# Attention, gate and mixer on one core: token products that wait for the token weights alone, and the second head's block first in the products with v

## The chip, the cores and the metric

The kernel runs on one core of one Trainium2 chip. The metric is the time of one execution on the device in microseconds (us); the median of three runs is given. The core has five engines with a program each: TensorE (PE in the rows, with PEld for its weight loads), VectorE (DVE), ScalarE (ACT), GpSimd (POOL) and SyncE (SP). They run side by side and wait for each other on semaphores.

## The reference

Three layers follow one another, in float32, for 4 batches of 576 tokens. Attention with 8 heads of dimension 64 keeps the 32 largest scores of each row:

```python
    scores = scale * np.matmul(q, k.transpose(0, 1, 3, 2))
    kth = np.partition(scores, -top_k, axis=-1)[..., -top_k:-top_k + 1]
    mask = scores >= kth
    ...
    return np.matmul(attn, v).astype(np.float32)
```

The gate layer multiplies a sigmoid of a causal convolution of five taps with x @ w_val, and the product with w_out. The mixer turns each value by an angle, mixes over tokens with two 576 x 576 matrices, and adds a channel product:

```python
    theta = x @ w_theta
    cos_t, sin_t = (np.cos(theta), np.sin(theta))
    zr = x * cos_t
    zi = x * sin_t
    yr = np.einsum('ts,bsd->btd', w_tok_r, zr)
    yi = np.einsum('ts,bsd->btd', w_tok_i, zi)
    y = yr + yi
    u = x + y
    return (u + np.maximum(u @ w_ch, 0.0)).astype(np.float32)
```

## The kernel before

**Tiles.** The heads go in 16 head pairs, four to a batch. Tokens are cut into two column parts, 256 and 320 wide (x or h is 0 or 1 in the names), and the 512 channels into four panels of 128 (m or c). An attention tile is 128 rows of one head. For each: score products (`ps`, L545 and L546), a copy to SBUF (`s`, L559), the search for the 32nd largest value on DVE (`cand`, `tops`, `thrs`; L581 to L608) with POOL's `y` (L602) and ACT's `n` (L594) in it, the exponential (`e`, L202), the masked product (`s`, L661), and transposes (`pt`, L674) copied to `pT` (L693).

**The product with v.** When both heads of a pair have their pT for a column part, `close` issues the block `px` (L757 to L765): five products for each head, the first head's result in rows 0 to 63 and the second's in rows 64 to 127 of one PSUM tile. The inner loop takes the first head (j = 0) and then the second for each 128 tokens. Then `close` multiplies px by the reciprocal row sums (`rs`, L718; spread as `rb`) into `xT`, and for batches 0 to 2 builds the convolution `gp` (L818 to L830: one step on ACT, one on POOL at L822, the rest on DVE).

**Gate and mixer.** They are written as Python generators that yield after each small group of products, and a step loop calls them. `front(b)` makes `pval` (x @ w_val, consumed by DVE at L859), `px2t`, the angles `pth` and the turned `z`. `back(b)` makes the token products `py` (L1114), adds them to x in `x2T` (L1093, in `y_out`), then the channel products `ph`, and stores. Each step of the loop gives the generators a budget of PE time (4150 ns). A generator that yields "sync" ends the work of that step. `later` and `mid` are lists of functions that run at fixed points of the next step.

**Splits.** Batches from 1 on, and w_ch for batch 0 too, use operands that are split into a high and a low part. `halve` does it: a cast on ACT (L408) and in the next round a subtract on DVE or POOL (L412). `want(b, name, m)` starts it for the weight panels up to m. `halve_room` does it for whole tiles: `X` (xT for pval), `G`, `U` (the output of the token products, for ph). For batch 1's first X the function `h_out` of `back(0)` starts the split of panel m as soon as that panel of ph is done and the head pair's xT is there; `front(1)` starts those that are missing.

**Weights.** The raw weights come as 64-bit words and are converted in 54 pieces, in the order conv, val, out, theta, tok, ch. `lacking[name]` counts the pieces that are left. The first line of `back` that runs is

```python
        while any(lacking.values()):
            yield "sync"
```

**What sets the order.** The loop runs the named stages of a step in a listed order. On DVE and ACT the instructions run in the order in which they are written. On PE, POOL and SP a scheduler orders them by priority and by when it expects their inputs.

Of the kernel before, what the change touches and what calls it, by code (L numbers as in the profile page):

```python
# [90 lines left out]
def mixer(ctx, tc, qT, kT, vt, w_val, conv_t, w_out, w_theta, w_tok, w_ch, out, flag):  # L91
# [99 lines left out]
    taken, lacking = set(), {}  # L191
# [63 lines left out]
    def double(u, j, x):  # L255

        r = slice(64 * j, 64 * j + 64)
        q2 = q2s[j]
        kh, kl = (io.tile([P, S], I32, tag=f"{t}{j}", name=f"{t}{j}_{u}_{x}") for t in ("kh", "kl"))
        for d in range(2):  # L260
            o = slice(64 * d, 64 * d + 64)
            nc.sync.dma_start(kh[o, :], raws["k", u, x][0][r, :].bitcast(I32))
            nc.sync.dma_start(kl[o, :], raws["k", u, x][1][r, :].bitcast(I32))
            q = raws["q", u, x][d][r, :].bitcast(I32)
            c = columns_of("q", x)
            if j and c.stop == S:
                nc.sync.dma_start(q2[o, c.start : NF * P], q[:, c.start : NF * P])
                nc.sync.dma_start(q2[o, S:], q[:, NF * P :])
            else:
                nc.sync.dma_start(q2[o, c], q[:, c])  # L270
        heads[u, j] = tuple(t.bitcast(F32R) for t in (q2, kh, kl))
# [123 lines left out]
    def chunk(b, x, what, c):  # L395
        both = parts_of(b, x, what)
        w = COLS[x][1] - COLS[x][0]
        return both[:, 0, c, :w], both[:, 1, c, :w]
# [6 lines left out]
    def halve(hi, lo, src, key, also=None):  # L405

        def higher():
            nc.scalar.copy(hi, src)  # L408
            later.append(lower)

        def lower():
            engine(key).tensor_tensor(lo, src, hi.bitcast(F32), ALU.subtract)  # L412
            if also is not None:
                also()
            if PATIENT and attending[0]:
                later.append(lambda: done.add(key))
            else:
                done.add(key)

        mid.append(higher)  # L420

    def halve_room(b, x, what, src):

        both = parts_of(b, x, what)
        lo, hi = COLS[x]
        for c in range(0, NC, 2):
            halve(both[:, 0, c : c + 2, : hi - lo], both[:, 1, c : c + 2, : hi - lo], src[:, c : c + 2, lo:hi],
                  (what, b, c, x))
        if what == "L" and x:
            halve(both[:, 0, :, hi - lo :], both[:, 1, :, hi - lo :], src[:, :, NF * P :], (what, b, "last", x))  # L430

    def halved(b, x, what):
        return [(what, b, c, x) for c in range(0, NC, 2)] + [(what, b, "last", x)] * (what == "L" and x)
# [7 lines left out]
    def place(k, m):  # L441

        if k < 3 or k % 3 == 2:
            return [ml.tile([P, DM], F32R if k < 3 else I32, tag=f"{t}{m}", name=f"{t}{m}_{k}") for t in ("hi", "lo")]
        if (k, 0) not in places:
            names = ("val", "out") if k % 3 == 0 else ("theta", "ch")
            for t in range(2):
                places[k, t] = cp.tile([P, NC, DM], I32, tag=f"w_{names[t]}", name=f"w{t}_{k}")
        return [places[k, t][:, m, :] for t in range(2)]
# [3 lines left out]
    def want(b, name, last=NC - 1):  # L453

        k = PHASES.index((b, name)) if b else -1
        if k > 2:
            return
        for m in range(last + 1):
            if (b, name, m) in mats:
                continue  # L460
            src = W[name][:, m, :] if name == "theta" else W[name][:, :, m * P : (m + 1) * P]
            both = place(k, m)
            mats[b, name, m] = both
            stored[name, m] = dp.tile([P, 2, DM], I32, name=f"{name}{m}")

            def store(both=both, to=stored[name, m]):
                for t in range(2):
                    nc.sync.dma_start(to[:, t, :], both[t].bitcast(I32))

            hi, lo = (t if name == "theta" else t.rearrange("p (c w) -> p c w", c=NC) for t in both)  # L470
            halve(hi, lo, src, ("w", b, name, m), store)
# [11 lines left out]
    def used(b, name):  # L483

        if b:
            k = PHASES.index((b, name))
            for k in {0: (), 1: (3,), 2: (4, 5)}.get(k, (k + 3,)):
                bring(k)

    def mat(b, name, m, c):  # L490
        return tuple(t[:, c * P : (c + 1) * P] for t in mats[b, name, m])
# [7 lines left out]
    def after(*keys):  # L499
        while not done.issuperset(keys):  # L500
            yield "sync"
# [6 lines left out]
    def products(ps, terms):  # L508

        last, w = len(terms) - 1, ps.shape[-1]  # L510
        for i, (a, b) in enumerate(terms):
            ways = passes(a, b)
            for k, (x, y) in enumerate(ways):
                n = x.shape[-1]
                for o in range(0, P, n):
                    nc.tensor.matmul(ps[o : o + n], x, y, start=(i + k == 0),  # L516
                                     stop=(i == last and k == len(ways) - 1), skip_group_check=(n < P))
            owe[0] += w * (1.275 if len(ways) > 1 else 1.675)
            if owe[0] >= GRAIN and i < last:
                yield paid()  # L520
# [3 lines left out]
    def paid():  # L524
        ns, owe[0] = owe[0], 0.0
        return ns
# [181 lines left out]
    def close(part):  # L708

        u, x = part["u"], part["x"]  # L710
        b, hp = divmod(u, NP)
# [47 lines left out]
        owed[0] -= 8.3 * w  # L759
        px = ps_m.tile([P, w], F32, tag="m", name=f"px_{u}_{x}")  # L760
        for c in range(NF + 1):
            for j in range(2):
                d = slice(64 * j, 64 * j + 64)
                of_v, k = (v[:, c, d], j * NF + c) if c < NF else (v_last[:, d], 2 * NF)
                nc.tensor.matmul(px[d, :], of_v, pT[:, k, :],  # L765
                                 start=(c == 0), stop=(c == NF), skip_group_check=True)
# [31 lines left out]
        if hp == NP - 1:  # L798
            jobs.append(front(b, (x,) if split else (0, 1)))
            if x:  # L800
                jobs.append(back(b))
# [284 lines left out]
    def back(b):  # L1086
        x2T = ms.pop(b)

        def y_out(m, h, ps):
            lo, hi = COLS[h]  # L1090

            def f():
                nc.vector.tensor_tensor(x2T[:, m, lo:hi], ps, x2T[:, m, lo:hi], ALU.add)  # L1093
                if m == NC - 1 and (h or b == B - 1):
                    for k in (h,) if b == B - 1 else range(2):
                        halve_room(b, k, "U", x2T)
                if not h:
                    want(b, "ch", m)
            return f

        while any(lacking.values()):
            yield "sync"
        if b < B - 1:
            for h, m in [(h, m) for h in range(2) for m in range(NC)]:
# [36 lines left out]
        def h_out(m, h, ps):  # L1141
            lo, hi = COLS[h]

            def f():
                nc.vector.scalar_tensor_tensor(x2T[:, m, lo:hi], ps, 0.0, x2T[:, m, lo:hi], ALU.max, ALU.add)
                n = b + 1
                if h and n in THREE:
                    want(n, "val", m)
                    if (n * NP + m, 0) in there:
                        split_x(n, m, 0)  # L1150
                done.add(("o", b, m, h))
            return f
# [8 lines left out]
        def turned(tiles):  # L1161
            for i in tiles:
                w = P if i < NF else REM
                po = ps_m.tile([P, NC, P], F32, tag="m", name=f"po_{b}_{i}")
                for c in range(NC):
                    nc.tensor.transpose(po[:w, c, :], x2T[:, c, i * P : i * P + w], ident)
                later.append(store(i, w, po))
                yield 450

        for h, m in [(h, m) for h in range(2) for m in range(NC)]:  # L1170
            lo, hi = COLS[h]
            yield from after(*halved(b, h, "U"), ("w", b, "ch", m))
            ps = ps_m.tile([P, hi - lo], F32, tag="m", name=f"ph_{b}_{m}_{h}")
            yield from products(ps, [(mat(b, "ch", m, c), chunk(b, h, "U", c)) for c in range(NC)])
            later.append(h_out(m, h, ps))
            if (h, m) == (1, NC - 1):
                used(b, "ch")
            yield paid()
            if h and m == 1:
                yield from after(*[("o", b, c, 0) for c in range(NC)])  # L1180
                yield from turned([0, 1])
# [65 lines left out]
    for k, part in enumerate(order):  # L1247
# [7 lines left out]
        elif split or x == 0:  # L1255
            when = (i0 - 7, i0 - 5, i0 - 5, i0 - 4, i0 - 3) if split or i0 and order[k - 1]["x"] and order[k - 1]["u"] // NP in SPLIT else (i0 - 9, i0 - 8, i0 - 7, i0 - 6, i0 - 3)
            a = (u, x if split else None)
            for step, do in zip(when, (load_heads, split_high, split_low, *(
                    lambda u, x, j=j: double(u, j, x) for j in range(2)))):
# [37 lines left out]
    def begin_close(i):  # L1297
        e = seq[i]
        if e is e.part["tiles"][-1]:
            chains.append(close(e.part))  # L1300
# [103 lines left out]
```

## Time and profile before

| | |
|---|---|
| median of three runs | 838.05 us (836.03 to 838.68) |
| the profiled execution | 838.7 us, of which 836.9 us are the span shown |
| granted TensorE clock, mean | 0.969 of full speed |
| PE busy | 734.5 us (88%) |
| DVE busy | 677.7 us (81%) |
| ACT busy | 639.4 us (76%) |
| POOL busy | 440.5 us (53%) |

Busy shares are of the span. Several engines are busy most of the time, so the time is set by chains that pass from one to the other; the busy share of an engine does not say whether it is the one that is waited for.

### The profile page before, as it was taken

How to read it: one execution, taken by the hardware profiler on the slowest of the kernel's cores; microseconds unless marked ns; L12 is line 12 of the kernel's file. 1: busy time of each engine (PE TensorE's matmuls, PEld its weight loads, DVE VectorE, ACT ScalarE, POOL GpSimd, SP SyncE). 2: the span in 40 equal slices, each digit the busy share in tenths (PEclk: the TensorE clock that was granted, in tenths of full speed). 3: DMA queues.
4: the chain of work that ended last, by engine and by line, in shares of the span. 5: the costliest groups of instructions: out<-in, count | busy, mean ns of one | idle time of the engine just before them, and what ended most of it. 6: DMA issues, size and time to landing. Idle time of an engine off the chain costs nothing.

```text
span 836.9 us, 15761 instructions
## 1 busy us (share of the span) xinstructions
PE 734.5 (88%) x4478; PEld 584.1 (70%) x4478; DVE 677.7 (81%) x2786; ACT 639.4 (76%) x1573; POOL 440.5 (53%) x583
## 2 busy tenths in 40 slices
PE   4476889968899899898699989999989899999995
PEld 3244667535665676697587777778988767898895
DVE  6999999979987889999899879989998685353522
ACT  6678898889788777989789888889987785346511
POOL 5876665545643536557677735547796143004600
PEclk9999899979999899999899989999999999999998
DMA  5566666635440253437455543234753300070002
GB/s 167 147 159 194 165 171 168 179 94 129 119 108 15 47 156 82 101 93 224 112 179 168 151 138 84 45 84 112 193 166 119 101 1 15 1 231 28 2 1 61
DMA packets 73601, 94.35 MB, mean 113 GB/s; under 512 B 13728, under 2 KB 37152, under 8 KB 73504
## 3 DMA queue, kind: packets, MB, share of 16 engines
q1 hardware_dynamic: 73184, 92.82, 40.8%
q8 instruction: 38, 0.62, 0.3%
q10 hardware_dynamic: 320, 0.43, 0.2%
q14 instruction: 59, 0.48, 0.2%
HBM read 49.96 MB, written 13.11 MB: 75 GB/s over the span
## 4 chain that ended last, share of the span: by engine, by line
PE 39%; DVE 32%; ACT 13%; POOL 6%; issue 5%; DMA 4%; SPq 0%; ACTq 0%; POOLq 0%
PE py L1114 8%; DVE cand L581 7%; DVE thrs L608 5%; PE px L765 5%; DVE s L661 4%; PE pth L516 4%; PE ph L516 3%; PE px2t L516 3%; PE pval L516 3%; PE py L1133 3%; DVE cand L587 3%; DVE tops L585 3%; PE pt L674 3%; ACT n L594 2%; POOL y L602 2%
## 5 line engine op out<-in xcount | busy, mean ns | idle before, releaser
L602 POOL TENSOR_TENSOR y<-s,n 128x576 f32<-128x576 f32 x144 | 190.9, 1325 | 158.1 <-DVE thrs L608 116.0
L581 DVE MAX8 cand<-s 128x8 f32<-128x96 f32 x864 | 211.4, 245 | 1.0 <-ACT s L559 1.0
L661 DVE SCALAR_TENSOR_TENSOR s<-s,thrs,e 128x576 f32<-128x576 f32 x144 | 137.7, 956 | 9.7 <-ACT e L202 9.7
L594 ACT ACTIVATE n<-s,tops 128x576 bf16<-128x576 f32 x144 | 112.1, 779 | 40.3 <-POOL y L602 18.8
L559 ACT ACTIVATE s<-ps 128x256 f32<-128x256 f32 (+1 forms) x288 | 103.1, 406 | 26.2 <-PE ps L737 10.3
L1114 PE MATMUL py<-w_tok,z 128*128 128x256 f32 (+1 forms) x432 | 118.8, 416 | 1.7 <-DVE z L973 1.7
L674 PE MATMUL pt<-ident,s 128*128 128x128 f32 x576 | 95.3, 286 | 28.4 <-ACT pT L693 15.4
L608 DVE MAX8 thrs<-y 128x8 f32<-128x584 f32 x144 | 109.5, 760 | 8.3 <-POOL y L603 8.0
L202 ACT ACTIVATE e<-s,least 128x576 f32<-128x576 f32 x144 | 110.9, 770 | 0.5 <-DVE s L661 0.4
L674 PEld LDWEIGHTS pt<-ident,s 128*128 128x128 f32 x576 | 69.0, 145 | 56.5 <-ACT pT L693 25.9
L545 PE MATMUL ps<-kh_None,q 128*128 128x256 f32 x240 | 92.0, 390 | 5.2 <-ACT rb L744 2.5
L1114 PEld LDWEIGHTS py<-w_tok,z 128*128 128x128 f32 x432 | 79.6, 195 | 22.3 <-DVE z L973 2.5
L765 PE MATMUL px<-pT,v 128*64 128x256 f32 (+1 forms) x512 | 84.5, 431 | 10.1 <-ACT pT L693 10.1
L693 ACT COPY pT<-pt 128x512 f32<-128x512 f32 x128 | 73.2, 572 | 24.4 <-PE pt L674 13.4
L585 DVE MAX8 tops<-cand 128x8 f32<-128x48 f32 x432 | 83.3, 193 | 0.1
L546 PE MATMUL ps<-kl_None,q 128*128 128x256 f32 x240 | 71.5, 301 | 0.0
L765 PEld LDWEIGHTS px<-pT,v 128*64 128x64 f32 x512 | 37.1, 141 | 43.4 <-issue 12.5
L545 PEld LDWEIGHTS ps<-kh_None,q 128*128 128x128 f32 x240 | 46.7, 195 | 20.2 <-ACT s L559 8.3
L545 PE MATMUL ps<-kh,q 128*128 128x256 f32 (+1 forms) x80 | 35.7, 454 | 24.3 <-ACT s L559 11.0
L587 DVE MATCH_REPLACE8 cand<-tops,cand 128x48 f32<-128x48 f32 x288 | 55.5, 193 | 0.0
L546 PEld LDWEIGHTS ps<-kl_None,q 128*128 128x128 f32 x240 | 47.1, 196 | 2.3 <-issue 0.9
L682 ACT COPY pT<-ps 64x128 f32<-64x128 f32 (+1 forms) x160 | 39.4, 246 | 12.0 <-PE ps L678 5.6
(215 smaller groups left out, 1742.2 us busy)
## 6 DMA issues: line engine op xcount, KB each, us to landing
kh_None<-kh_None SPq DMA_DIRECT2D x48, 144.0 KB, 2.6
kl_None<-kl_None SPq DMA_DIRECT2D x48, 144.0 KB, 2.7
v<-in_vt_dram SPq DMA_DIRECT2D x20, 256.0 KB, 3.4
out_dram<-x2T SPq DMA_DIRECT2D x16, 256.0 KB, 3.4
w<-ch SPq DMA_DIRECT2D x16, 256.0 KB, 4.1
w<-theta SPq DMA_DIRECT2D x16, 256.0 KB, 5.6
raw_hi<-in_w_tok_dram SPq DMA_DIRECT2D x14, 256.0 KB, 4.1
kh<-kh SPq DMA_DIRECT2D x24, 144.0 KB, 2.5
```

What stands on the lines that cost most here:

```text
L202: ins = nc.scalar.activation(out, src, func, **more).ins
L516: nc.tensor.matmul(ps[o : o + n], x, y, start=(i + k == 0), stop=(i == last and k == len(ways) - 1), skip_group_check=(n < P))
L545: nc.tensor.matmul(bank[:, :w], q2, kh[:, lo:hi], start=(j == js[0]), stop=False)
L546: nc.tensor.matmul(bank[:, :w], q2, kl[:, lo:hi], start=False, stop=(j == js[-1]))
L581: nc.vector.max(d["cand"][:, k, 8 * x : 8 * x + 8], s_tiles[i][:, x * SUB : (x + 1) * SUB])
L594: nc.scalar.activation(n, s_tiles[i], AF.Sign, bias=d["tops"][:, k, KC - 1 : KC], scale=-(1.0 + 2.0 ** -22), accum_out=acc)
L602: nc.gpsimd.tensor_tensor(y[:, :S], s_tiles[i], d.pop(("n", k)), ALU.mult)
L608: nc.vector.max(thrs[:, N - 1 - i : N - 1 - i + NK], d.pop(("y", k)))
L661: nc.vector.scalar_tensor_tensor(p, p, thr(i), e.exp, ALU.is_ge, ALU.mult, accum_out=part["sums"][:, e.slot : e.slot + 1])
L674: nc.tensor.transpose(e.pt[:, c, :], p[:, c * P : (c + 1) * P], ident)
L765: nc.tensor.matmul(px[d, :], of_v, pT[:, k, :], start=(c == 0), stop=(c == NF), skip_group_check=True)
L1114: nc.tensor.matmul(ps, z[:, m * P : (m + 1) * P], W["tok"][:, w, lo:hi], start=(i + k == 0), stop=(i == NF))
```

## The change

Three edits. In `close` the inner loop over the two heads runs second head first. In `back` the wait at the start is for the token weights alone instead of all weights. The split of w_ch panels, which `y_out` starts after each of the first four token outputs, is put off in `due` as long as pieces of w_ch are unconverted, and caught up before the channel products, which wait for the rest of w_ch.

```diff
@@ close @@
         for c in range(NF + 1):
-            for j in range(2):
+            for j in (1, 0):
                 d = slice(64 * j, 64 * j + 64)
@@ back, y_out @@
                 if not h:
-                    want(b, "ch", m)
+                    due.append(m)
+                    while due and not lacking["ch"]:
+                        want(b, "ch", due.pop(0))
             return f
 
-        while any(lacking.values()):
+        due = []
+        while lacking["tok"]:
             yield "sync"
@@ back, ahead of the channel products @@
+        while lacking["ch"]:
+            yield "sync"
+        while due:
+            want(b, "ch", due.pop(0))
         for h, m in [(h, m) for h in range(2) for m in range(NC)]:
```

The order listings below show three places. Numbers behind a name's underscore count tiles and differ between the two programs. "x2" is the same instruction twice.

The first is PE around the px block of head pair 10 in batch 2 (first column part; v_10 is its v, pT_0 its transposed weights, py the token products of batch 1, ps the scores), at 505 us in the trace of before. Before:

```order
L1114 MATMUL py_1_0_6726<-w_tok,z_1_6511 128x256
L765 MATMUL px_0_6780<-pT_0_6243,v_10_0_6662 64x256
L1114 MATMUL py_2_0_6777<-w_tok,z_0_6374 128x256
L765 MATMUL px_0_6780<-pT_0_6243,v_10_0_6662 64x256 x2
L545 MATMUL ps_0_6770<-kh_11_None,q_88 128x256
...
L546 MATMUL ps_256_6774<-kl_11_None,q_88 128x320
L765 MATMUL px_0_6780<-pT_0_6243,v_10_0_6662 64x256 x5
L765 MATMUL px_0_6780<-pT_0_6243,v_last 64x256 x2
```

Of the change:

```order
L1117 MATMUL py_1_0_6726<-w_tok,z_1_6511 128x256
L1117 MATMUL py_2_0_6777<-w_tok,z_0_6374 128x256 x2
L765 MATMUL px_0_6780<-pT_0_6243,v_10_0_6662 64x256 x2
L545 MATMUL ps_0_6770<-kh_11_None,q_88 128x256
...
L765 MATMUL px_0_6780<-pT_0_6243,v_10_0_6662 64x256 x6
L765 MATMUL px_0_6780<-pT_0_6243,v_last 64x256 x2
```

The first px product stood alone between two py products and the block was cut into 1, 2 and 7; now the py products stand together and the block is cut into 2 and 8.

The second is ACT at the casts of U of batch 0 (x2T is the token output), at 352 us in the trace of before. Before:

```order
L744 COPY rb_1_4308<-ps_256_4485 128x192
L594 ACTIVATE n_4530,acc_4529<-s_4373,tops_4450 128x576
L247 CAST kh_None<-kl_None 128x576
L247 CAST qh_None<-ql_None 128x576
L202 ACTIVATE e_4563<-s_4204,least 128x576
L408 CAST U_0_4527<-x2T_1800 128x512 x2
L408 CAST U_1_4528<-x2T_1800 128x2x320 x2
L693 COPY pT_1_4466<-pt_4515 128x4x128
```

Of the change:

```order
L559 ACTIVATE s_4434<-ps_0_4386 128x256
L559 ACTIVATE s_4434<-ps_256_4391 128x320
L682 COPY pT_0_4370<-ps_0_4386 64x128
L725 COPY rT<-ps_0_4386 5x128
L202 ACTIVATE e_4467<-s_4087,least 128x576
L408 CAST U_0_4440<-x2T_1800 128x512 x2
L408 CAST U_1_4441<-x2T_1800 128x2x320 x2
L693 COPY pT_0_4370<-pt_4429 128x4x128
```

The casts moved ahead by two tiles, behind the e of an earlier tile, and on DVE the U subtracts moved with them.

The third is POOL at the X subtracts of batch 1 (xT of the four head pairs are 3178, 3751, 4280 and 4833 before, 3178, 3754, 4283 and 4894 in the change; X_0 is the first column part, X_1 the second), at 399 us in the trace of before. Before, all four X_0 subtracts stand among the tiles ahead of this:

```order
L617 TENSOR_SCALAR least<-tops_5072 128x6
L412 TENSOR_TENSOR X_1_5228<-xT_3178,X_1_5228 128x320
L412 TENSOR_TENSOR X_1_5228<-xT_3751,X_1_5228 128x320
...
L412 TENSOR_TENSOR X_1_5228<-xT_4280,X_1_5228 128x320
L769 MEMSET xT_6791 128x4
L412 TENSOR_TENSOR X_1_5228<-xT_4833,X_1_5228 128x320
L769 MEMSET xT_7295 128x4
L602 TENSOR_TENSOR y_5337<-s_5034,n_5219 128x576
L603 TENSOR_TENSOR y_5337<-steps,acc_5218 128x8
L822 TENSOR_TENSOR gp_5207<-gp_5207,ct_1_1_5269 128x576
```

Of the change:

```order
L412 TENSOR_TENSOR X_0_4775<-xT_4894,X_0_4775 128x256
L412 TENSOR_TENSOR X_1_5226<-xT_3178,X_1_5226 128x320
L617 TENSOR_SCALAR least<-tops_5093 128x6
L412 TENSOR_TENSOR X_1_5226<-xT_3754,X_1_5226 128x320
...
L412 TENSOR_TENSOR X_1_5226<-xT_4283,X_1_5226 128x320
...
L412 TENSOR_TENSOR X_1_5226<-xT_4894,X_1_5226 128x320
L769 MEMSET xT_7295 128x4
L602 TENSOR_TENSOR y_5297<-s_5071,n_5217 128x576
L603 TENSOR_TENSOR y_5297<-steps,acc_5216 128x8
L822 TENSOR_TENSOR gp_5205<-gp_5205,ct_1_1_5255 128x576
```

The fourth X_0 subtract stands in the same run of instructions as the X_1 subtracts, ahead of the gp step. On PE the last quarter of pval_0, pval_1 and pval_2 of the first column part reads it, and pval_3 of that part, which stood ahead of the first piece of pval_0 of the second part, stands behind the px block of head pair 8.

## Rows read from the trace of the kernel before

**Rows 1.** The page, parts 1, 4, 5 and 6 (one row of each).

```profile
PE 734.5 (88%) x4478; PEld 584.1 (70%) x4478; DVE 677.7 (81%) x2786; ACT 639.4 (76%) x1573; POOL 440.5 (53%) x583
...
PE 39%; DVE 32%; ACT 13%; POOL 6%; issue 5%; DMA 4%; SPq 0%; ACTq 0%; POOLq 0%
...
L765 PE MATMUL px<-pT,v 128*64 128x256 f32 (+1 forms) x512 | 84.5, 431 | 10.1 <-ACT pT L693 10.1
...
kl_None<-kl_None SPq DMA_DIRECT2D x48, 144.0 KB, 2.7
```

**Rows 2.** Busy time by stretch; behind POOL the granted clock, DMA share, GB/s.

```profile
490.00:560.00 70.00, 70.00 (x402) 53.99 (x399) 63.41 (x285) 59.20 (x142) 35.52 (x46) 0.96 0.30 71
...
340.00:360.00 20.00, 16.96 (x113) 14.05 (x112) 18.02 (x74) 18.07 (x46) 10.63 (x14) 0.91 0.30 74
400.00:420.00 20.00, 14.41 (x91) 11.98 (x90) 16.41 (x75) 13.55 (x35) 12.15 (x19) 0.83 0.42 109
```

**Rows 3.** Chain in order of time, 505 to 511 us: start, us, what.

```profile
505.19 0.57 PE px L765 x2
505.77 0.63 PE py L1114 x2
506.40 0.58 PE px L765 x4
...
510.27 0.87 PE py L1114 x4
```

**Rows 4.** Chain in order of time, 546 to 550 us.

```profile
546.71 2.31 PE px L765 x20
```

**Rows 5.** Chain in order of time, 345 to 357 us.

```profile
352.71 3.68 DVE U L412 x4
```

**Rows 6.** Timelines, 340 to 358 us: start, busy us, instruction [idle before <-releaser].

```profile
345.21 0.59 ACT L693 COPY pT<-pt 128x512 f32<-128x512 f32 x1 [1.89 <-PE pt L674]
...
352.04 2.42 ACT L408 CAST U<-x2T 128x512 fp32r<-128x512 f32 x4
...
352.71 3.68 DVE L412 TENSOR_TENSOR U<-x2T,U 128x512 fp32r<-128x512 f32 x4 [1.94 <-ACT U L408]
...
350.99 1.41 POOL L253 TENSOR_TENSOR kl_None<-kl_None,kh_None 128x576 fp32r<-128x576 f32 x1 [1.40 <-ACT kh_None L247]
```

**Rows 7.** Timeline of DVE, 293 to 295 us.

```profile
293.63 0.69 DVE L412 TENSOR_TENSOR lo_-1_3724<-w_ch,hi_-1_3723 128x512 fp32r<-128x512 f32 x1 [0.89 <-ACT hi_-1_3723 L408]
```

**Rows 8.** Timelines of PE, DVE and POOL, 396 to 411 us.

```profile
408.39 0.63 PE L516 MATMUL pval<-X,hi 128*128 128x320 f32 x1 [4.90 <-DVE gp L859]
...
398.94 0.41 DVE L859 SCALAR_TENSOR_TENSOR gp<-gp,pval 128x256 f32<-128x256 f32 x1
...
406.27 1.67 DVE L830 SCALAR_TENSOR_TENSOR gp<-xT,w_conv,gp 128x576 f32<-128x576 f32 x2 [3.55 <-POOL gp L822]
...
399.08 1.71 POOL L412 TENSOR_TENSOR X<-xT,X 128x320 fp32r<-128x320 f32 x2
...
401.22 0.87 POOL L412 TENSOR_TENSOR X<-xT,X 128x320 fp32r<-128x320 f32 x1
...
402.10 1.34 POOL L412 TENSOR_TENSOR X<-xT,X 128x320 fp32r<-128x320 f32 x1
...
404.83 1.40 POOL L822 TENSOR_TENSOR gp<-gp,ct 128x576 f32<-128x576 f32 x1
```

**Rows 9.** Chain in order of time, 406 to 430 us.

```profile
408.03 0.32 DVE gp L859
...
409.02 0.21 PE ps L545
...
410.41 2.40 PE pval L516 x9
...
426.41 1.75 PE pval L516 x12
...
428.54 0.34 ACT s L559
```

## The prediction

> **What bounds the kernel now.** I read the page first: TensorE is busy for 88% of the span, yet it holds only 39% of the chain that ended last, VectorE 32%, ScalarE 13%, GpSimd 6% [rows 1]. So no engine is the limit everywhere, and each edit has to be priced in its own stretch. The table by stretch comes next. From 490 to 560 us TensorE is busy all the time (70.00 of 70), and the same stretch of the next batch, from 676 on, repeats it: TensorE time saved there is time saved. From 340 to 360 it is busy for 16.96 of 20 while VectorE and ScalarE have 18.02 and 18.07. From 400 to 420 it is busy for 14.41 of 20, at a granted clock of 0.83; what runs out there is something that it waits for [rows 2].
>
> **The px pairs.** One px block is ten products of 64 output rows, five per head, and each product leaves two records, so 20 records are a block. A block that runs uninterrupted takes 2.31 us, that is 0.46 us for a pair of products [rows 4]. In the block at 505 us the first product stands alone (x2) and takes 0.57 us, while two products (x4) right behind take 0.58: a product without its partner costs as much as a pair [rows 3]. The order of before has 13 of 32 blocks with such an odd first run, because the first head's share of pT was ready ahead of the second head's; in the order of the change all 32 are cut into even runs. Where TensorE is the limit, at 505 and in the same form at 676, the change takes out the lone slot (0.57) and the interruption of py: the py product between took 0.63 us, against 0.87 for two of them (0.43 each) [rows 3], so 0.20 more. That is 0.77 for each block, −1.54 together. The other odd blocks lie where TensorE is not the limit, or their lone product runs ahead of a wait (the one of the block at 412 stands at 397, ahead of the wait for gp), so I give them nothing. Bounds: 0, if the pair merely waits for the later head where the lone product did not, and −6.0 (13 x 0.46) if every slot counts. px waits for pT for 10.1 us in all [rows 1], and a pair now needs the later half of it; the scheduler puts the pair behind the py product that stood behind the lone one, so that cover is still there. **Term 1: −1.54 (−6.0 to 0).**
>
> **The token gate.** Batch 0's first token product keeps its place on TensorE, behind the same score products, and the split of w_ch is not later either: by the order its four casts stand where they stood, one a step earlier. What moves is behind it: from the fourth column panel on, batch 0's products run about one step ahead, and the cast and subtract of U (token output, made for w_ch) stand two steps ahead on ScalarE and VectorE. From the third val panel of batch 1 on the orders are the same again. So the change acts between about 290 and 430 us, and outside it only through the pairs.
>
> **U.** Before, the chain runs from e through the first U cast to four U subtracts (3.68 us) [rows 5]; VectorE waited 1.94 us for the cast [rows 6]. After, the casts stand two steps ahead, in front of a pT copy at 345.21 for which ScalarE waited 1.89 us [rows 6]. So the casts fill idle time of ScalarE, and VectorE meets the subtracts with their casts done. The two idle times agree: the gain is 1.94. It is 0 if ScalarE's wait is needed elsewhere; since four casts take 2.42 us [rows 6], 0.53 more than the wait, the pT copy can be 0.53 late, which is the upper bound. The subtracts themselves may be shorter. A subtract of w_ch of 512 columns, with GpSimd at rest, took 0.69 us [rows 7]; by columns (2304 in all) the four would take 3.10, and they took 3.68 with two GpSimd subtracts (kl and ql, the first of them 1.41 us) in the same time [rows 6]. Two steps earlier those two are not beside them: up to 0.58 more. I don't count it, since y of GpSimd may stand there instead. **Term 2: −1.94 (−2.52 to +0.53).**
>
> The Trainium skill, SBUF — State Buffer, "Who interferes with whom", says that a VectorE instruction with two SBUF inputs contends with a GpSimd instruction that reads SBUF, as it fetches its second input through the interface that both share. The 3.68 against 3.10 agrees. By that rule term 2 would be −2.52 with GpSimd idle beside U, and −1.94 or less with a y there; it is part of rival B.
>
> **GpSimd's burst.** U earlier makes ph earlier, and with it x2T of panel 3 and the splits of batch 1's X. Before, all four subtracts of X_0 stood among earlier steps. After, h_out reaches panel 3 before head pair 7 has left its xT, so the fourth X_0 subtract falls into the burst of X_1 subtracts ahead of gp L822. The burst is on the path: gp L822 starts at 404.83, VectorE waited 3.55 us for it, then gp L830, the reciprocal, and gp L859, for which TensorE waited 4.90 us [rows 8]. The four X_1 subtracts of 320 columns took 1.71 (two), 0.87 and 1.34 us [rows 8], 0.98 in the mean, so one of 256 columns is 0.78 (0.70 to 1.07). Also, the last quarter of pval_0 waits for that subtract, so pval_0's L859, at 398.94 in VectorE's spare time before, comes behind gp L830: 0.32 us [rows 9] that is uncovered now. **Term 3: +1.10 (0.70 to 1.40).**
>
> **pval_3_0.** It ran ahead of TensorE's wait; after, it stands behind px of head pair 8, in the stretch from 408.39 to 428.54 in which TensorE sets the end. A panel of 12 products of 320 columns takes 1.75 us there, so 256 columns take 1.40; at the lower clock of 410.41 (nine products in 2.40) it would be 2.56. Against it stand three score products of 0.21 us, 0.63 together, which now run within the wait, because the first piece of pval_0_1 no longer blocks TensorE, and 0.32 us because TensorE goes on at the reciprocal and not at L859 [rows 9]. I take the full clock: 413 and later is there already. **Term 4: +0.45 (−0.95 to +1.61).**
>
> The next load of kl and ql moves behind output stores on SP's queue; ScalarE reached its cast with no wait, after the work on other tiles that hides the load, so I cost it at nothing. If that cover is gone, the next heads' scores wait for at most one load, which lands 2.7 us after its issue [rows 1].
>
> **Sum.** −1.54 − 1.94 + 1.10 + 0.45 = −1.93, from 838.7 for the profiled execution: 836.8. The median of the runs, 838.05, is 0.65 below the profiled one, so I forecast 836.1. About 0.3%, 2.5 us, is what a measurement of this kernel can tell from no change; faster begins at 835.5, slower at 840.6.
>
> **Rivals.**
> - A, forecast, chance 0.47: the sum, 834.5 to 839.
> - B, faster, chance 0.25: the odd slots count in half of the 13 blocks (−3.0), U gives its 2.52, and pval_3_0 hides (−0.95); with +1.10 that is −5.4: 832.7, and 834 with term 4 as I have it. For it: TensorE has the largest share of the chain, and the wait of 4.90 us at 408 is large. Against: the burst stays, and the reciprocal that TensorE needs stands behind gp L830 in either order.
> - C, slower, chance 0.15: GpSimd's burst lengthens the wait of 4.90 us, and TensorE then works at its lower clock for longer. After the wait of 4.90 the products up to 412.81 have 0.27 us for 320 columns, against 0.146 at 426 (1.75 for 12) [rows 9]: the granted clock is at the lower of its two levels (1.2 and 2.4 GHz) for 4.4 us. A stretch of L us more at half rate loses L/2; it must last 9 us longer, to 422, to undo the 1.93 and cost 2.5 beside it. At 10 us: 841.1. Against it: TensorE has more to do in the wait than before.
> - D, no effect, chance 0.13: the first product keeps its place, the two ends of the moved stretch are fixed by GpSimd's burst, and the pairs lie under other waits: 838.05.
>
> **How the numbers follow.** Faster holds B and the lower part of A (0.12): 0.37. Same holds the rest of A and nearly all of D: 0.46. Slower is C and a little of D: 0.17. The terms' ends add to −8.8 and +3.5, which would be 829.3 to 841.6; I take 831 to 841, which leaves out two ends that need every bound to be met at once.
>
> **What would show it.** Right: every px group has a number of records divisible by four, the blocks at 505 and 676 are 0.77 us shorter, VectorE's wait for the U cast is gone and U stands near 345, one GpSimd X subtract of 256 columns stands within 2 us ahead of gp L822, which comes about as late as before, and TensorE's 4.90 us wait ends at the reciprocal. Wrong: TensorE waits for pT ahead of the pairs for longer than 10.1 us; the stretch 340 to 360 is as long as before (ScalarE was the limit); or the stretch behind 408 lasts over 2 us longer.

## The result, and the profile after

The changed kernel takes 830.71 us (median of four runs, 830.42 to 831.85) against 838.14 before (four runs): a ratio of 0.9913, with a 95% interval of 0.99 to 0.9926. Run again later beside two experiments it took 830.59 us, ratio 0.9905 (0.9889 to 0.9922). So it is faster by 7.4 us. The forecast was 836.1, with a range down to 831.0: the sign was right, the gain 5.4 us too small, and the time lies just outside the range.

The page of the changed kernel, with the rows that answer to [rows 1]:

```profile
PE 724.5 (87%) x4478; PEld 579.8 (70%) x4478; DVE 674.6 (81%) x2786; ACT 639.1 (77%) x1573; POOL 438.8 (53%) x583
...
PE 41%; DVE 31%; ACT 13%; POOL 5%; issue 5%; DMA 4%; SPq 0%; ACTq 0%; POOLq 0%; DVEq 0%
...
L765 PE MATMUL px<-pT,v 128*64 128x256 f32 (+1 forms) x512 | 77.7, 440 | 12.7 <-ACT pT L693 12.7
```

TensorE is busy 10.0 us less, of which px gives 6.8 (84.5 to 77.7): the lone slots are gone. px waits for pT longer than before, 12.7 us against 10.1. The prediction had named just that as a sign of failure; the time fell all the same, and the chain shares hardly moved.

At the block of head pair 10, the chain of the changed kernel in order of time (start, us, what) answers to [rows 3]:

```profile
500.24 0.58 PE px L765 x4
...
501.66 1.88 PE px L765 x16
...
504.13 0.86 PE py L1117 x4
```

The lone x2 of 0.57 us is gone and py runs at 0.43 us for a product. Before, the way from the first px product to the end of the block took 4.49 us (505.19 to 509.68) with one py product inside; now it takes 3.30 (500.24 to 503.54), with 0.43 for that py ahead: 0.76 less, where the prediction had 0.77.

At U, the timelines of DVE, ACT and POOL of the changed kernel answer to [rows 6]:

```profile
341.89 2.77 DVE L412 TENSOR_TENSOR U<-x2T,U 128x512 fp32r<-128x512 f32 x4
...
341.06 2.38 ACT L408 CAST U<-x2T 128x512 fp32r<-128x512 f32 x4
...
345.49 1.28 POOL L602 TENSOR_TENSOR y<-s,n 128x576 f32<-128x576 f32 x1 [3.42 <-DVE cand L581]
```

The wait of 1.94 us has no successor, and the subtracts take 2.77 us in place of 3.68. GpSimd is at rest for most of that time.

At GpSimd's burst, the timelines of POOL, DVE and PE of the changed kernel, and one row of its chain (the last), answer to [rows 8, 9]:

```profile
392.32 2.07 POOL L412 TENSOR_TENSOR X<-xT,X 128x256 fp32r<-128x256 f32 x2
...
399.39 1.40 POOL L822 TENSOR_TENSOR gp<-gp,ct 128x576 f32<-128x576 f32 x1
...
400.82 1.67 DVE L830 SCALAR_TENSOR_TENSOR gp<-xT,w_conv,gp 128x576 f32<-128x576 f32 x2 [3.90 <-POOL gp L822]
...
402.64 0.37 PE L722 MATMUL ps<-ident,rs 128*4 128x128 f32 x1 [4.38 <-DVE rs L718]
...
408.96 1.43 PE pval L516 x12
```

The fourth X_0 subtract stands in the burst (0.72 us of the 2.07; the rest is the first X_1 subtract), VectorE waits 3.90 us instead of 3.55, TensorE waits for the reciprocal, and pval_3_0 takes 1.43 us behind px, the price that the prediction had from the full clock. This is as predicted but for one sign: the X_0 subtract opens the burst, 7.07 us ahead of gp L822, and not within 2 us of it.

To see where the lead comes from, I take the start of VectorE's search `thrs` (L608) of each attention tile, 144 in a program and in one order in all of them, and subtract that of the kernel before; both counted from the first tile, which starts 16 us into the span (the rows of profiles count from the span's start). Each column is the change of this difference (us) in a stretch: from 77 to 269 us (tiles 17 to 55, up to the first token product), from 269 to 436 (tiles 55 to 91, with U and the burst), and from 503 to 683 us (tiles 105 to 143). Negative is ahead of before. Each line is one profiled execution; the kernels are those of the next section.

```
kernel          77-269  269-436  503-683
changed          -2.71    -2.51    -2.78
changed_again    -2.10    -2.09    -1.62
px_only          -0.39    +1.52    -2.13
gate_only        +1.01    -1.66    -0.60
px_early         -3.19    +0.70    -0.60
px_late          +1.13    +0.54    -2.12
gate_px_late     +0.96    -2.07    -0.99
px_not5          -1.88    +0.80    -2.78
px_not58         -0.60    +0.03    -0.23
u_late           -0.48    +0.96    -2.16
x1_dve           -0.83    -5.26    -2.78
px_ghost         +1.57    -1.88    -2.78
px_shift6        -1.15    -2.65    -2.17
x_late           -2.82    -1.45    +0.56
x12_dve          -0.62    -5.63    -2.33
px_shift         -0.81    -1.15    -1.04
```

The first column also holds executions that differ by themselves: changed and u_late run the same instructions in one order up to the token products and differ by 2.2 us there. So that column is read by groups. The ten with pairs in that stretch (px_ghost, px_shift6 and px_shift aside) have -1.56 in the mean, the four with the lone products (the kernel before, which is 0, gate_only, px_late and gate_px_late) +0.78.

### The profile page after: what moved, and what is told of

It is laid out like the page before. It is cut to its first block, busy times and chain, and to the rows that moved or that the text cites. A ratio compares the mean times of both kernels' runs of the same rounds, so it can differ in the third digit from the quotient of the medians.

```text
span 829.2 us, 15756 instructions
## 1 busy us (share of the span) xinstructions
PE 724.5 (87%) x4478; PEld 579.8 (70%) x4478; DVE 674.6 (81%) x2786; ACT 639.1 (77%) x1573; POOL 438.8 (53%) x583
## 4 chain that ended last, share of the span: by engine, by line
PE 41%; DVE 31%; ACT 13%; POOL 5%; issue 5%; DMA 4%; SPq 0%; ACTq 0%; POOLq 0%; DVEq 0%
PE py L1117 7%; DVE cand L581 7%; PE px L765 7%; DVE thrs L608 5%; PE pth L516 4%; PE px2t L516 4%; PE ph L516 4%; DVE s L661 3%; PE pval L516 3%; PE py L1136 3%; PE pt L674 3%; DVE cand L587 3%; DVE tops L585 2%; DVE gp L830 2%; PE ps L545 2%
## 5 line engine op out<-in xcount | busy, mean ns | idle before, releaser
L602 POOL TENSOR_TENSOR y<-s,n 128x576 f32<-128x576 f32 x144 | 188.4, 1308 | 164.3 <-DVE thrs L608 117.2
L661 DVE SCALAR_TENSOR_TENSOR s<-s,thrs,e 128x576 f32<-128x576 f32 x144 | 135.5, 941 | 10.2 <-ACT e L202 10.2
L1117 PE MATMUL py<-w_tok,z 128*128 128x256 f32 (+1 forms) x432 | 115.6, 409 | 3.4 <-DVE z L973 3.4
L608 DVE MAX8 thrs<-y 128x8 f32<-128x584 f32 x144 | 109.5, 760 | 6.2 <-POOL y L603 5.9
L765 PE MATMUL px<-pT,v 128*64 128x256 f32 (+1 forms) x512 | 77.7, 440 | 12.7 <-ACT pT L693 12.7
L765 PEld LDWEIGHTS px<-pT,v 128*64 128x64 f32 x512 | 34.7, 145 | 43.6 <-ACT pT L693 15.4
```

What stands on the lines that cost most here:

```text
L602: nc.gpsimd.tensor_tensor(y[:, :S], s_tiles[i], d.pop(("n", k)), ALU.mult)
L608: nc.vector.max(thrs[:, N - 1 - i : N - 1 - i + NK], d.pop(("y", k)))
L661: nc.vector.scalar_tensor_tensor(p, p, thr(i), e.exp, ALU.is_ge, ALU.mult, accum_out=part["sums"][:, e.slot : e.slot + 1])
L765: nc.tensor.matmul(px[d, :], of_v, pT[:, k, :], start=(c == 0), stop=(c == NF), skip_group_check=True)
L1117: nc.tensor.matmul(ps, z[:, m * P : (m + 1) * P], W["tok"][:, w, lo:hi], start=(i + k == 0), stop=(i == NF))
```

## The experiments

Each time stands beside one of the kernel before, taken with it (838.5 to 838.8 us), and the ratio is to that.

**px_only: the first edit alone.**

```diff
-            for j in range(2):
+            for j in (1, 0):
```

> Only the first edit: second head's block first in px, the token gate as before. My prediction's term 1: two blocks in TensorE-bound stretches count, about -1.5 us against 838.1, so 836.6. The rival after the result (every lone px slot counts, covered or not, about 0.4 us for each of 13): about -5.2 us, 833. If the whole change comes from the gate: 838.

836.42 us, ratio 0.9971 (0.996 to 0.9981). That is what term 1 alone would give, and it looks as if the prediction's px part held. The next runs show that the early blocks alone, to which the prediction gave nothing, give as much; in the trace of px_only a loss of 1.52 us between 269 and 436 us stands against its gains (see the table).

**gate_only: the other two edits alone**, px as before (their first lines; the rest as in the change).

```diff
-        while any(lacking.values()):
+        due = []
+        while lacking["tok"]:
...
-                    want(b, "ch", m)
+                    due.append(m)
+                    while due and not lacking["ch"]:
+                        want(b, "ch", due.pop(0))
```

> Only the second and third edit: token products wait for the token weights alone, w_ch split put off; px as before. My prediction's terms 2 to 4: -0.4 us, 837.7. From the trace of the changed kernel (lead over before grows from 2.7 to 5.2 us between the first token product and 450 us): -2.5 us, 835.6.

835.58 us, ratio 0.9961 (0.9947 to 0.9975): 3.2 us, where terms 2 to 4 gave 0.4.

**px_early and px_late: the px order for a part of the head pairs.**

```diff
-            for j in range(2):
+            for j in ((1, 0) if u < 6 else (0, 1)):
```

and the other way round in px_late.

> Second head first in px for the first six head pairs only (before the first token product; 8 of the 13 blocks with a lone product), token gate as before. My prediction: none of these is on the path, so 838.1. Rival, every lone slot counts 0.4 us: -3 us, 835.1.

> Second head first in px for head pairs 6 to 15 only (5 of the 13 blocks with a lone product), token gate as before. My prediction: -1.5 us, 836.6. Rival, every lone slot counts 0.4 us: -2 us, 836.1; from the lead of the changed kernel after 500 us (5.2 to 7.9): -2.7 us, 835.4.

px_early 835.95, ratio 0.9971 (0.9961 to 0.9981); px_late 837.55, ratio 0.9988 (0.998 to 0.9997). The early blocks, to which the prediction gave nothing, are worth some 2.4 us; the late ones, on which it rested, 1.0 by the ratio and 1.2 by the medians.

**gate_px_late: the changed kernel without the early px blocks.**

```diff
-            for j in (1, 0):
+            for j in ((0, 1) if u < 6 else (1, 0)):
```

> The changed kernel, but the first six head pairs keep the first head first (8 of the 13 blocks with a lone product are back, all but the last two of them before the first token product). Theory after the first runs, that these lone slots count although TensorE is not the limit there: about 2.5 to 3 us above the changed kernel, 833.5. My prediction's step, that they cost nothing: 831, no difference from the changed kernel.

834.4 us, ratio 0.994 (0.9927 to 0.9953): 3.7 above the changed kernel by the medians, 2.3 to 2.9 by the ratios. With the gate as without it, the early blocks count.

**px_not5 and px_not58: the px order alone, without one or two head pairs**, to test whether places where its trace lost time explain why the two halves add to 0.9971 x 0.9961 = 0.9932 and the whole is 0.9913.

```diff
-            for j in range(2):
+            for j in ((0, 1) if u == 5 else (1, 0)):
```

with `u in (5, 8)` in px_not58.

> The px order alone (token gate as before), without head pair 5, at whose first block the px order alone lost 1.15 us in the trace. If that loss explains why the two halves of the change together gain more than they do apart: 835.2, 1.2 below the px order alone (836.4). If the sum differs for another reason: 836.4 or, with two lone products more, 837.

> The px order alone, without head pairs 5 and 8, where its traces lose 1.15 us (331 us) and some 0.9 us (403 to 436 us). If these two losses are why the halves of the change add to less apart than together: 834.5, 1.9 below the px order alone. If not: 836.4.

835.46 us, ratio 0.9963 (0.995 to 0.9976), and 835.8 us, ratio 0.9963 (0.9949 to 0.9976). Both intervals overlap that of px_only, and the second exception brought nothing. This is inconclusive: the gap of 0.19% is about as large as the intervals of its parts.

**px_shift: an extra slot written into each of the 32 blocks.** A slot is the time of a pair. The second head's block runs first and the first head's follows one place behind, so that the first and the last product have no partner.

```diff
-        for c in range(NF + 1):
+        for c in range(NF + 2):
             for j in (1, 0):
+                e = c - (1 - j)
+                if not 0 <= e <= NF:
+                    continue
```

(e replaces c in the lines behind.)

> The changed kernel, with the first head's block one place behind the second's in each px block: the first and the last product of each of the 32 blocks have no partner, six slots for five. At 0.46 us for a slot TensorE is busy 14.7 us longer. If a slot counts in full everywhere: 845. If a slot counts by what the 13 slots of the change gave in early and late parts (about 0.3 us each): 840. If only slots where TensorE is the limit count, some 10 of 32: 835.

833.84 us, ratio 0.9945 (0.9932 to 0.9958): 3.1 us above the changed kernel. Its chain at the block that took 2.31 us in [rows 4], and at the block of head pair 10:

```profile
543.50 2.36 PE px L768 x20
...
503.13 1.01 PE px L768 x6
...
504.97 1.88 PE px L768 x14
```

A block that runs in one piece, as 18 of the 32 do, takes 0.05 us more, so most of the extra slots hardly show. A block that score products cut takes 2.89 us (1.01 and 1.88) where the changed kernel takes 2.46 (0.58 and 1.88), 0.43 more. So 3.1 us stand against 14 slots that show, 0.2 each: the rival that each slot counts in full (0.46) falls; that about half of it counts is not excluded.

**px_ghost, px_shift6, and the changed kernel again: place or slot.** px_ghost adds to the changed kernel one product ahead of each early block, whose result the block overwrites:

```diff
+        if u < 6:
+            nc.tensor.matmul(px[:64, :], v[:, 0, :64], pT[:, 0, :], start=True, stop=True, skip_group_check=True)
         for c in range(NF + 1):
```

px_shift6 is px_shift for `u < 6` alone.

> The changed kernel, with one product more ahead of each px block of the first six head pairs: the first head's first product, issued as soon as its pT is there and overwritten by the block. By the order it stands where the lone products of before stand; the block behind it stays in pairs. If a lone product costs by its place, ahead of scores that are waited for: most of the 3 to 3.7 us that the lone products of these head pairs cost, 833.5. If what costs is the broken pairing behind it: 831.

> The changed kernel, with the first head's block one place behind the second's for the first six head pairs only: six slots for five in these blocks, and no product ahead of the block. If the slot costs (0.46 us each): eight of them 3.7 us, 834.4. If the place costs and the slot does not: 831.

> The changed kernel once more, on the same chip as the two others: 830.7 if its first time holds, and the reference for them.

px_ghost 835.45, ratio 0.9963 (0.9948 to 0.9977); px_shift6 831.72, ratio 0.992 (0.99 to 0.9939); the changed kernel 830.59. Twelve products ahead of their blocks cost 4.9 us with all pairs intact; the slots inside the blocks cost 1.1, within the intervals. The two do not add the same work: eight of the twelve blocks of px_shift6 are cut and so show their slot, and TensorE is busy 2.7 us longer there (727.2 to 724.5), 6.5 us longer in px_ghost (731.0). Seven of the twelve products of px_ghost stand apart from their block, as seven of the eight lone products of before do; the other five stand directly at it. So the place counts beside the slot, but the two runs do not give each its price.

What the place does is seen only in part. The timelines of TensorE around 200 us, first in the changed kernel (run again), then in px_ghost (the line numbers of the block differ by the added lines):

```profile
196.11 0.43 PE L545 MATMUL ps<-kh_None,q 128*128 128x256 f32 x1
...
199.71 0.39 PE L545 MATMUL ps<-kh_None,q 128*128 128x256 f32 x1 [0.60 <-ACT s L559]
```

```profile
196.99 0.44 PE L545 MATMUL ps<-kh_None,q 128*128 128x256 f32 x1
...
198.32 0.75 PE L762 MATMUL px<-pT,v 128*64 128x320 f32 x2
199.01 0.81 PE L516 MATMUL pval<-xT,w_val 128*128 128x320 f32 x2
...
200.60 0.39 PE L545 MATMUL ps<-kh_None,q 128*128 128x256 f32 x1
```

The scores behind the early product come 0.89 us later than in the changed kernel, but those ahead of it were 0.88 later already: at this place the product costs nothing. It does bring other work forward: val products that stand at 207 and 209 us in the changed kernel run here at 199 to 202. Some 15 us on, the two differ in the clock. Stretches and timelines of the changed kernel (run again), then of px_ghost; a row of a stretch has the busy us of TensorE, of its weight loads, of VectorE, ScalarE and GpSimd, then the granted clock, the DMA share and GB/s:

```profile
207.00:214.00 7.00, 5.32 (x35) 4.22 (x34) 6.93 (x30) 6.83 (x20) 3.49 (x7) 1.00 0.37 115
214.00:220.00 6.00, 6.00 (x30) 4.49 (x29) 5.96 (x20) 4.11 (x12) 5.04 (x5) 1.00 0.43 108
...
213.72 0.70 PE L516 MATMUL pval<-xT,w_val 128*128 128x320 f32 x2
```

```profile
207.00:214.00 7.00, 4.48 (x32) 3.53 (x30) 6.93 (x37) 6.82 (x20) 3.76 (x6) 0.95 0.37 122
214.00:220.00 6.00, 5.67 (x17) 4.62 (x18) 6.00 (x19) 4.72 (x12) 5.46 (x5) 0.50 0.19 59
...
214.81 1.27 PE L516 MATMUL pval<-xT,w_val 128*128 128x320 f32 x2
```

In px_ghost TensorE has less to do from 207 to 214 us (4.48 us against 5.32) and then runs at the lower of its two levels (0.50, that is 1.2 GHz; 1.00 is 2.4). By the starts of `thrs`, px_ghost loses 1.94 us here, of 3.67 in all up to the first token product. The other executions agree: from 214 to 220 us the clock was 1.00 in changed, changed_again, px_early, px_not5 and x_late, which lose nothing against each other; 0.72 in before, px_only, px_late, px_not58, u_late, x1_dve and x12_dve, which lose 0.5 to 0.8; 0.50 in gate_only, gate_px_late and px_ghost, which lose 1.9. (At 1.00 too, px_shift6 loses 0.2 here and px_shift 1.7, in another way.) Of the 2.3 us between the groups of the first column some 0.9 arise here. But the order alone does not set the clock: x1_dve runs the same instructions in the same order as changed_again up to there, was busy for 5.33 us from 207 to 214, and had 0.72. A further 0.93 of the 3.67 us comes at the blocks of 242 and 257 us, where the extra product stands directly at the block and counts in full. So place, slot and clock all have a part, and no run here takes them apart; nor was it tested whether it matters that an early product also claims the block's PSUM tile earlier.

**u_late: the changed kernel with U's split two steps later.**

```diff
-                    for k in (h,) if b == B - 1 else range(2):
-                        halve_room(b, k, "U", x2T)
+                    def split():
+                        for k in (h,) if b == B - 1 else range(2):
+                            halve_room(b, k, "U", x2T)
+                    if b:
+                        split()
+                    else:
+                        later.append(lambda: later.append(split))
```

> The changed kernel with the split of U of batch 0 put off by two steps, so that from U on ScalarE, VectorE, GpSimd and TensorE run in the order of before; token products and px as in the change. If terms 2 to 4 of my prediction hold (-1.94 + 1.10 + 0.45): 0.4 us above the changed kernel, 831.1. By the traces (U gains 3.0, the burst and pval_3_0 cost 1.4): 1.6 above, 832.3. If the gate's gain does not come from U at all: 830.7.

835.33 us, ratio 0.9963 (0.995 to 0.9976): 4.6 above the changed kernel. So the gate's gain comes from U's place, and the earlier token products alone bring nothing that shows. Its chain at U:

```profile
351.42 0.52 ACT U L408
...
351.96 3.69 DVE U L412 x4
```

The cast and the 3.69 us of subtracts are back. By the starts of `thrs`, its lag behind the changed kernel grows by 3.25 us from 322 to 366 us (tiles 68 to 78, counted from the first tile; gate_only, with the changed order there, keeps its lag within 0.02). Half of that, 1.62, is time that VectorE stands idle. The other half, 1.64, is instructions of VectorE that take longer: U's subtracts 0.93 and four subtracts of w_val's split 1.10, against 0.49 less for the masked products. The timelines of DVE and POOL of the kernel before, which shares this, and of DVE of the changed kernel (the last row):

```profile
377.26 1.83 DVE L412 TENSOR_TENSOR lo<-w_val,hi 128x512 fp32r<-128x512 f32 x2
...
377.35 1.19 POOL L412 TENSOR_TENSOR X<-xT,X 128x256 fp32r<-128x256 f32 x1
...
366.07 1.28 DVE L412 TENSOR_TENSOR lo<-w_val,hi 128x512 fp32r<-128x512 f32 x2
```

A GpSimd subtract of X stood beside these too, and in the changed kernel it does not. Behind 366 us u_late can't price the burst and pval_3_0 apart: it has no X_0 subtract in the burst, but its pval_3_0 stands behind px as in the changed kernel, not where it stood before, which the expectation had not foreseen.

**x_late: no early splits of batch 1's X.** The two lines in `h_out` that start them are left out.

```diff
-                    if (n * NP + m, 0) in there:
-                        split_x(n, m, 0)
```

> The changed kernel, without the early splits of batch 1's X in the output of the channel products: three more X subtracts fall into GpSimd's burst ahead of the gp step. Term 3 of my prediction (0.8 us for each subtract in the burst): 2.4 us above the changed kernel, 833.1. If the burst is not on the path: 830.7.

837.48 us, ratio 0.9987 (0.9978 to 0.9997). The expectation left out that these lines serve batches 2 and 3 too. In the starts of `thrs` it goes from 0.58 ahead of the changed kernel at 377 to 1.75 behind at 386, 2.3 us for three subtracts in the burst, 0.78 each, as expected; 0.99 behind is left at 422; another 3.3 come behind 563 us, at later batches.

**x1_dve and x12_dve: X subtracts on VectorE.** The X_1 subtracts of batch 1 go to VectorE, where it waits for gp; in x12_dve those of batch 2 too.

```diff
     def engine(key):
+        if key[0] == "X" and key[1] == 1 and key[3] == 1:
+            return nc.vector
```

> The changed kernel with the four X_1 subtracts of batch 1 on VectorE, where it waits 3.9 us for gp, instead of in GpSimd's burst. If the burst sets the wait (term 3): the burst is 2.6 us of X_1 shorter and y comes behind gp, VectorE works 1.9 us in its wait, so 2 us below the changed kernel, 828.7. If the wait has another cause, or VectorE is the limit there: 830.7 to 832.5.

> As before it, but the X_1 subtracts of batch 2 on VectorE too. If the same wait stands in batch 2: 1 to 2 us below the kernel with batch 1 alone, 827. If not, 1.9 us of work for VectorE more: 829.5 to 832.

x1_dve 829.03 us, ratio 0.9887 (0.9867 to 0.9906), and x12_dve 828.87, ratio 0.9882 (0.9862 to 0.9902). Both beat the kernel before clearly and the changed one by some 1.6 us, with intervals that overlap a little; the second adds nothing that can be told from the first. The timelines of DVE, POOL and PE of x1_dve:

```profile
394.87 1.69 DVE L414 TENSOR_TENSOR X<-xT,X 128x320 fp32r<-128x320 f32 x4
...
396.27 1.57 POOL L824 TENSOR_TENSOR gp<-gp,ct 128x576 f32<-128x576 f32 x1
...
401.42 0.27 PE L724 MATMUL ps<-ident,rs 128*4 128x128 f32 x1 [0.31 <-DVE rs L720]
```

Four subtracts take VectorE 1.69 us, gp starts at 396.27 and not 399.39, and TensorE's wait of 4.38 us for the reciprocal is 0.31. The burst was on the path, as term 3 had it.

## Why the prediction was wrong, point by point

**Term 1, the pairs, where TensorE is the limit: right.** 0.76 us at the block of 505 us for 0.77 predicted. Over the stretch from 503 us the twelve lines of the table that have the late pairs in all blocks (x_late aside, whose later batches changed, and px_shift) gain 2.07 in the mean, the three without them (before, gate_only, px_early) 0.40: 1.67 for 1.54 predicted. By the times the late pairs give 1.0 to 1.8 (px_late; gate_px_late against gate_only).

**Term 1, the rest: this step failed.** The sentence was "The other odd blocks lie where TensorE is not the limit, or their lone product runs ahead of a wait [...], so I give them nothing." The early blocks gave 2.3 us in the traces (+0.78 against -1.56) and, in the times, 2.4 (px_early) to 3.7 (gate_px_late). I had asked at each block whether its slot was covered. But a lone product ahead of its block also moves other products (px_ghost), and that showed in other places: at 214 us in the clock, at 242 and 257 us as slots that counted in full. That the lone products cost time is shown; how much of it comes which way stays open.

**Term 2, U: the wait right, the rest missing; this step failed too.** Forecast -1.94 (-2.52 to +0.53). From 318 to 380 us (tiles 66 to 80) the changed kernel gains 3.72 on the one before, 3.75 when run again, gate_only 3.52. VectorE is idle 1.97 less, which is the wait as forecast; its instructions take 1.74 less, and this I had counted as nothing. The prediction had named up to 0.58 of it: U's subtracts became 0.91 us shorter (3.68 to 2.77). It had not seen that w_val's subtracts would lose their GpSimd neighbours too (1.09). The reason that I gave for the longer U subtracts, GpSimd's kl and ql subtracts in the same time, agrees with the rows after. With no kl and ql beside them they are even shorter than the 3.10 worked out from columns. The Trainium skill, SBUF — State Buffer, "Who interferes with whom", tells of this contention; the traces agree with it (2.77 against 3.68 us).

**Terms 3 and 4, the burst and pval_3_0: right together.** Forecast +1.10 and +0.45. From 380 to 436 us (tiles 80 to 91) gate_only, which has px as before, loses 1.39 on the kernel before, for 1.55; the changed kernel loses 0.74, and 1.21 when run again. For term 3, x_late gives 0.78 for a subtract in the burst, the price that I had, and x1_dve shows the wait go when the burst goes; VectorE's own wait grew by only 0.35 (3.55 to 3.90). For term 4 the scores run in the wait and TensorE goes on at the reciprocal, as told, and pval_3_0 takes 1.43 us for the 1.40 in the sum. No run takes the two terms apart.

**The sum.** Terms 2 to 4 were -0.39 and measured -3.2 (gate_only) to -4.6 (u_late) in the times; the early blocks were 0 and measured -2.4 to -3.7; the late ones were -1.54 and measured -1.0 to -1.8. Rival B had the right sign and, with 832.7 to 834, was nearest; it let half of the lone slots count, without saying which half, and counted the whole of U's shorter subtracts. Whether the two halves really add to some 1.6 us less than the whole stays open.

## What to carry to other kernels

An engine's wait near by need not cover an instruction placed ahead of it: other instructions move with it. Twelve extra px products ahead of their blocks cost 4.9 us, an extra slot written into the same blocks 1.1, and part of the difference came in other places than the products themselves. A split that depends on a late input can be worth more than its wait, since moving it also changes which instructions of the neighbouring engine run beside it: here 1.97 us of wait and 1.74 of shorter instructions. And when an engine waits for a burst on a slower one, look whether the waiting engine can do the burst itself: that alone gave some 1.6 us more.

## What was not expected of the hardware

VectorE's masked product takes 0.81 us, but 2.06 beside GpSimd's kl and ql subtracts, by the timelines of DVE and POOL of the changed kernel:

```profile
346.89 0.81 DVE L661 SCALAR_TENSOR_TENSOR s<-s,thrs,e 128x576 f32<-128x576 f32 x1
...
349.94 2.06 DVE L661 SCALAR_TENSOR_TENSOR s<-s,thrs,e 128x576 f32<-128x576 f32 x1
...
349.94 1.44 POOL L253 TENSOR_TENSOR kl_None<-kl_None,kh_None 128x576 fp32r<-128x576 f32 x1
```

So the contention that left U came back in part at the masked product, 1.25 us in one instruction.

One program, one order, two executions: the px block at 107 us of the changed kernel took 1.95 us in its first profile and 3.47 in the second. Behind each row of the timeline stands the row of its stretch; the column ahead of the DMA share is the granted clock.

```profile
107.22 1.95 PE L765 MATMUL px<-pT,v 128*64 128x256 f32 x16 [1.32 <-ACT pT L693]
...
107.00:109.50 2.50, 2.28 (x20) 1.46 (x20) 2.50 (x16) 2.46 (x9) 1.90 (x4) 1.00 0.69 147
```

```profile
107.84 3.47 PE L765 MATMUL px<-pT,v 128*64 128x256 f32 x16 [1.69 <-ACT pT L693]
...
107.00:110.00 3.00, 2.16 (x10) 1.25 (x12) 2.96 (x19) 2.96 (x10) 1.83 (x4) 0.59 0.68 144
```

The clock was at the higher of its two levels (2.4 GHz) in the one and mostly at the lower (1.2) in the other. Such steps are part of the 2.2 us by which executions of one order differ before the first token product, and a single trace can't tell a gain of that size there.
